# A new order for the opening of a fused attention and MLP kernel: the first split pair moves into it, two masks become two wide operations, the last store goes out in halves

## The chip, the cores and the metric

The kernel runs on one core of one Trainium2 chip. The metric is device time in microseconds (us) of one execution. Before the change the median of three runs is 651.92 us (651.72 to 652.86). The engines are called PE (TensorE, matmul), DVE (VectorE), ACT (ScalarE), POOL (GpSimd) and SP (SyncE, which here does nothing but issue DMAs); PEld is the weight load of PE.

## What is computed

Attention over 4 batches of 8 heads with 768 positions of 64 numbers, where a query sees the first 4 keys and a window of 128 keys back, and then a gated MLP on all 3072 tokens:

```python
scores = scale * np.matmul(q, k.transpose(0, 1, 3, 2))
keep = is_sink | in_window            # pos < n_sink, 0 <= rel < window
scores = np.where(keep, scores, -1000000000.0)
a = np.exp(scores - np.max(scores, axis=-1, keepdims=True))
a = a / (np.sum(a, axis=-1, keepdims=True) + 1e-09)
x = np.matmul(a, v)                   # then (3072, 512)
h = x @ w_in                          # 512 x 2048, float64 weights
g = h * np.clip(h + 3.0, 0.0, 6.0) / 6.0
out = (g @ w_out).astype(np.float32)  # 2048 x 512
```

`n_sink` and `window` are inputs. Where they exceed 16 and 128 a general path behind a branch at the kernel's end computes everything anew; with the values here the branch jumps over it.

## The kernel before

Work is cut into units of 256 positions of one batch (12 units, three of each batch) and pairs of heads, four to a unit, so that there are 48 pairs `s`. The first 16 pairs belong to the first unit of each batch. They are "plain": their scores are float32 matmuls on operands as loaded. The other 32 are "split": queries and keys are cut into a high and a low part (`split_parts`), and DMAs within the chip's own buffers stack the parts (`B_k`, `B_q`, eight DMAs a pair). A pair's steps are scores, masking and row minimum on DVE (`S_least`), exponential on ACT (`X_exp`), transposes on PE, a copy back on ACT or DVE (`T_copy`), and the product with the values (`E_plain`, `E_av`).

The MLP takes two units at once. Its 16 weight blocks are float64 in memory; each is loaded (`W_load`, 1 MB) and decoded in six steps of 128x1024 (`W_decode`): 1 and 2 on ACT, 3, 4 and 6 on DVE, 5 on the engine that a letter of `WHI` names. `PFE`, `XHS`, `XHF` and `GHF` name engines for other copies in the same way. Every product is made of three matmuls of 512 columns (high by high, high by low, low by high), `two_product` (line 690) and `two_second` (line 700) in six-matmul steps.

The opening is a list of some 900 steps written out, `FIRST`: p, q, u, l, v load, S are scores, M masking, X exponential, T transposes, C the copy, E the values, R, U, V, x, y the rest of a plain pair, W a weight load, w.j.k decode step k of block j, F, G and O the MLP of units 0 and 1 (products in, activation, products out), b the parts of x, i.n are n matmuls that nothing reads. Each engine, SP's DMA issue included, takes these steps in the order of the list. When a buffer that a DMA writes is still in use, SP stands at that DMA with all behind it.

After the list comes a loop of slots (line 872), one for each pair from `FROM` on. A slot's `ORDER` holds the steps of neighbouring pairs (c scores and softmax of the pair before, k and q splits of this one, d transposes, s sinks, e values of the pair two back, l and v loads) and eight letters f. Each f takes one six-matmul MLP step from a queue; a group of two units has 64 of them and eight pairs feed it. `SPARED` (line 861) takes f's out of a slot again: 2 of 8 from seven of the first nine slots, 1 from two. The scheduler may move instructions of the loop among each other; the opening stays as written.

The last steps are the four outputs of the last two units: ACT scales 128x512 out of PSUM (line 658), SP stores it (line 660). Then each engine reads a flag and jumps over the general path (line 904), and SP waits for all stores.

Of the kernel before, what the change touches and what calls it, by code (L numbers as in the profile page):

```python
# [44 lines left out]
def attn_ffn_kernel(ctx: ExitStack, tc: tile.TileContext, qx, kx, vx, px, vsx, limits, w_in, w_out, out):  # L45
    nc = tc.nc
    B, NU, NP = qx.shape[0:3]
# [46 lines left out]
    nc.sync.dma_start(out=raw.rearrange("p a b -> p (a b)"), in_=limits.bitcast(I32).partition_broadcast(P))  # L94
# [22 lines left out]
    def unless_sink(dst, bias):  # L117
        nc.vector.scalar_tensor_tensor(out=dst, in0=colf[:, 0:P], scalar=ns_f, in1=bias, op0=ALU.is_ge, op1=ALU.mult)
# [94 lines left out]
    GHF = "AADAAADADAAAADAD"  # L213
    WHI = "ADDDAADDDAADDDAD"
# [54 lines left out]
    PFE = "ADADDDDDDDADAAADDADDAADAAAAAAADA"  # L269
    XHS = "AAAAAAAADDADAAAA"  # L270
    XHF = "AAADADAAADADAAAA"
# [16 lines left out]
    def A_kq(s):  # L288
        b, u, p = pus[s]
        kr = work.tile([P, 400], F32, name="kr")  # L290
        qr = work.tile([P, UT], F32, name="qr")
        nc.sync.dma_start(out=kr[:, 0:ncol(u)], in_=kx[b, u, p, :, 0:ncol(u)])
        nc.sync.dma_start(out=qr, in_=qx[b, u, p])
        st_[s].update(kr=kr, qr=qr)

    def A_v(s):
# [7 lines left out]
        VS = work.tile([P, 3, 4 * D], F32R, name="VS")  # L304
        v4 = VS.rearrange("p s (h d) -> p s h d", h=4)
        vr = work.tile([P, 3, 2, D], F32, name="vr", bufs=1)
        nc.sync.dma_start(out=vr[:, 0:n], in_=vx[b, u, p, :, 0:n])
        split_parts(nc, v4[:, 0:n, 0::2, :], v4[:, 0:n, 1::2, :], vr[:, 0:n], nc.scalar, nc.vector)
        st_[s]["VS"] = VS

    def B_k(s):
# [6 lines left out]
        st_[s]["ktqt"], st_[s]["KQ"] = ktqt, work.tile([P, KQ], F32R, tag="K", name="K", bufs=1)  # L320
        K = st_[s]["KQ"][:, 0:1600].rearrange("p (h r w) -> p h r w", h=2, r=2)
        for h in range(2):
            for r in range(2):
                nc.sync.dma_start(out=K[D * r:D * (r + 1), h, :, 0:w].bitcast(F32),
                                  in_=kt[D * h:D * (h + 1), :, 0:w].bitcast(F32))
        st_[s]["K"] = K

    def B_q(s):
# [4 lines left out]
        split_parts(nc, qt[:, 0, :], qt[:, 1, :], d["qr"], eng(QHI, s), eng(QLO, s))  # L333
        Q = d["KQ"][:, 1600:KQ].rearrange("p (h t) -> p h t", h=2)
        for h in range(2):
            for r in range(2):
                nc.sync.dma_start(out=Q[D * r:D * (r + 1), h, :].bitcast(F32),
                                  in_=qt[D * h:D * (h + 1), r, :].bitcast(F32))
        d["Q"] = Q
# [309 lines left out]
    def ffn_out(tt, pool, acc, dst, final=False):  # L649
# [4 lines left out]
        elif pool is work:  # L654
            o = spare(0)[:, tt]
        else:
            o = pool.tile([P, DM], F32, name="ost")
        nc.scalar.mul(out=o, in_=acc, mul=1.0 / 6.0)
        if pool is work:
            nc.sync.dma_start(out=dst.rearrange("(s r) d -> r s d", s=2), in_=o)  # L660
        else:
            nc.sync.dma_start(out=dst, in_=o)

    def ffn_whole(x, pool, psum_h, psum_o, dsts):
# [11 lines left out]
        for tt in range(2):  # L676
            ffn_out(tt, pool, state[f"o{tt}"], dsts[tt])
# [15 lines left out]
    def two_second(n, j, one, state, tts=(0, 1)):  # L693
        gh, gl = (x.rearrange("p (t u) -> p u t", u=2)[:, one] for x in state[j])
        for tt in tts:
# [7 lines left out]
            if j == LAST - 1 and n:  # L703
                b, u = units[2 * n + one]
                r0 = b * S + u * UT + P * tt
                ffn_out(tt, work, acc, out[r0:r0 + P, :], 2 * n + one == len(units) - 1)
# [20 lines left out]
    def drain(n):  # L727
# [333 lines left out]
```

## Time and profile before

| | us |
|---|---|
| median of 3 runs | 651.92 |
| the profiled execution | 652.39 |
| its span, first to last instruction | 650.7 |
| PE busy | 640.5 (98%) |
| DVE busy | 491.3 (76%) |
| ACT busy | 414.6 (64%) |
| POOL busy | 180.0 (28%) |

The granted TensorE clock is 0.998 over the span, the upper of its two levels (2.4 GHz). Of the profiled execution, 1.7 us lie outside the span. A matmul's duration in the profile is longer than the step from one to the next, since they overlap, so a PE that is called busy can still lose time; how fast it goes is read from the count of matmuls in a stretch.

### The profile page before, as it was taken

Reading aid. Unit: us, or ns where it says so; the run is one execution under the profiler, and the core shown is the slowest. Engines: PE = TensorE matmul, PEld = TensorE weight load, DVE = VectorE, ACT = ScalarE, POOL = GpSimd, SP = SyncE. Lnnn points to the kernel's source line nnn. Section 1 sums busy time; section 2 is a strip of 40 time slices with the busy share of each in tenths; the row PEclk is TensorE's granted clock in tenths of the full one; section 3 lists DMA queues with packets and bytes.
Section 4 is the critical chain, followed back from the end, with each engine's and each line's share of the span. In section 5 each row is a group of like instructions: output and inputs, shape, how many; then the busy total and the mean of one; then the engine's idle time right before and its main releaser. Section 6 shows DMA issues by size and latency. Waiting matters only on the chain.

```text
span 650.7 us, 11572 instructions
## 1 busy us (share of the span) xinstructions
PE 640.5 (98%) x3556; PEld 574.3 (88%) x3556; DVE 491.3 (76%) x1290; ACT 414.6 (64%) x1046; POOL 180.0 (28%) x336
## 2 busy tenths in 40 slices
PE   8999999999999999999999999999999999999996
PEld 7898988888888889999998999999999999888885
DVE  5999999957887887977888878788788787433331
ACT  5978778645777788666777776678867765311111
POOL 1000000001454444454445434543354344000000
PEclk9999999999999999999999999999999999999999
DMA  8545940018665657544555555445754540100001
GB/s 320 208 172 215 380 154 1 2 56 212 169 164 138 177 137 205 142 116 120 128 139 145 169 132 136 117 116 137 196 129 104 121 105 2 64 1 1 0 2 70
DMA packets 45749, 82.93 MB, mean 127 GB/s; under 512 B 7024, under 2 KB 30832, under 8 KB 43632
## 3 DMA queue, kind: packets, MB, share of 16 engines
q1 hardware_dynamic: 45680, 82.11, 43.9%
q8 instruction: 31, 0.51, 0.3%
q14 instruction: 38, 0.31, 0.1%
HBM read 41.19 MB, written 6.29 MB: 73 GB/s over the span
## 4 chain that ended last, share of the span: by engine, by line
PE 92%; ACT 3%; DMA 2%; issue 1%; DVE 1%; SPq 0%; POOL 0%; ACTq 0%; DVEq 0%; POOLq 0%
PE o L700 35%; PE hps L690 34%; PE av L561 5%; PE sp L402 4%; PE av L532 3%; PE pt L496 2%; PE sp L371 2%; PE pt L478 2%; PE o L645 2%; PE hps L611 1%; DMA qr<-in_qx_dram 1%; ACT Pt L421 1%; PE idle L88 1%; DMA K<-kt 1%; DMA raw_s<-in_vsx_dram 1%
## 5 line engine op out<-in xcount | busy, mean ns | idle before, releaser
L690 PE MATMUL hps<-x,w 128*128 128x512 f32 x1104 | 263.5, 383 | 0.0
L700 PE MATMUL o<-w,gh 128*128 128x512 f32 x736 | 223.9, 384 | 0.0
L690 PEld LDWEIGHTS hps<-x,w 128*128 128x128 f32 x1104 | 201.1, 189 | 24.8 <-ACT xf L35 0.3
L700 PEld LDWEIGHTS o<-w,gh 128*128 128x128 f32 x736 | 137.3, 197 | 11.2 <-issue 0.3
L700 PE MATMUL o<-w,g 128*128 128x512 f32 x368 | 139.7, 380 | 0.0
L463 POOL TENSOR_TENSOR Pt<-Pt 128x256 f32<-128x256 f32 x64 | 53.5, 836 | 276.2 <-ACT Pt L421 276.2
L622 ACT ACTIVATE ost<-hps,three 128x512 f32<-128x512 f32 x80 | 54.9, 686 | 87.1 <-PE hps L690 86.5
L627 DVE SCALAR_TENSOR_TENSOR ost<-ost,hps 128x512 f32<-128x512 f32 x80 | 54.7, 684 | 55.9 <-ACT ost L622 55.1
L509 POOL TENSOR_SCALAR_AFFINE_SELECT ph<-ph 128x256 fp32r<-128x256 f32 x128 | 68.2, 534 | 54.9 <-ACT ph L35 54.8
L700 PEld LDWEIGHTS o<-w,g 128*128 128x128 f32 x368 | 72.4, 197 | 6.9
L384 DVE CUSTOM_DVE_ANT_0 Pt<-sp,m_t 128x272 f32<-128x272 f32 x128 | 53.5, 434 | 32.8 <-PE sp L402 26.9
L421 ACT ACTIVATE Pt<-Pt,nb 128x272 f32<-128x272 f32 x128 | 65.8, 514 | 13.2 <-DVE nb L384 12.9
L511 POOL TENSOR_SCALAR_AFFINE_SELECT ph<-ph 128x256 fp32r<-128x256 f32 x128 | 59.6, 466 | 35.1 <-DVE ph L30 29.6
L636 DVE TENSOR_TENSOR g<-ost,gh 128x512 fp32r<-128x512 f32 x80 | 65.4, 817 | 2.7
L409 ACT ACTIVATE Pt<-Pt,rc 128x144 f32<-128x144 f32 x128 | 46.0, 406 | 9.4 <-POOL Pt L463 4.7
L402 PE MATMUL sp<-K 128*128 128x272 f32 x256 | 41.8, 281 | 1.0 <-DMA K<-kt 0.4
L402 PEld LDWEIGHTS sp<-K 128*128 128x128 f32 x256 | 37.6, 190 | 3.8 <-issue 1.4
L561 PEld LDWEIGHTS av<-ph,VS 128*128 128x128 f32 x256 | 38.0, 190 | 3.2 <-issue 0.5
L561 PE MATMUL av<-ph,VS 128*128 128x256 f32 x256 | 39.0, 275 | 0.0
L41 DVE CAST gh<-ost 128x512 fp32r<-128x512 f32 x80 | 36.1, 452 | 2.5
L35 ACT ACTIVATE ph<-pt 128x256 fp32r<-128x256 f32 x64 | 24.6, 385 | 20.5 <-PE pt L496 19.6
L564 DVE TENSOR_TENSOR xf<-av,xf 64x256 f32<-64x256 f32 x64 | 26.6, 416 | 10.3 <-ACT xf L563 9.4
(107 smaller groups left out, 836.7 us busy)
## 6 DMA issues: line engine op xcount, KB each, us to landing
K<-kt SPq DMA_DIRECT2D x128, 200.0 KB, 3.5
K<-kt SPq DMA_DIRECT2D x128, 64.0 KB, 2.5
kr<-in_kx_dram SPq DMA_DIRECT2D x32, 200.0 KB, 2.5
vr<-in_vx_dram SPq DMA_DIRECT2D x32, 192.0 KB, 2.6
out_dram<-ost SPq DMA_DIRECT2D x22, 256.0 KB, 2.6
lent<-in_w_in_dram SPq DMA_DIRECT2D x5, 1024.0 KB, 9.2
qr<-in_qx_dram SPq DMA_DIRECT2D x40, 128.0 KB, 2.6
lent<-in_w_out_dram SPq DMA_DIRECT2D x5, 1024.0 KB, 9.6
```

The costliest lines, as they stand in the source:

```text
L384: nc.vector.tensor_tensor_reduce(out=cell(s, h, t, 0, w), in0=sp[:, 0:w], in1=m[:, 0:w], scale=-SCALE, scalar=3.0e38, op0=ALU.add, op1=ALU ...
L402: nc.tensor.matmul(out=sp[:, 0:w], lhsT=Q[:, h, t * P:(t + 1) * P], rhs=keys, start=(r == 0), stop=(r == 1))
L421: nc.scalar.activation(out=blk, in_=blk, func=AF.Exp, scale=-1.0, bias=d["nb"][:, i:i + 1], accum_out=d["sm"][:, i:i + 1])
L463: nc.gpsimd.tensor_tensor(out=both, in0=both, in1=prior, op=ALU.add)
L509: nc.gpsimd.affine_select(out=prior[i], in_=own[i], pattern=[[0, 2], [-1, P]], base=0, channel_multiplier=1, compare_op=ALU.is_gt, fill=0.0)
L511: nc.gpsimd.affine_select(out=own[i], in_=own[i], pattern=[[0, 2], [1, P]], base=0, channel_multiplier=-1, compare_op=ALU.is_ge, fill=0.0)
L561: nc.tensor.matmul(out=o, lhsT=l, rhs=r, start=(j == 0), stop=(j == len(seq) - 1))
L622: nc.scalar.activation(out=gf, in_=hp, func=AF.Relu, bias=three, scale=1.0)
L627: nc.vector.scalar_tensor_tensor(out=gf, in0=gf, scalar=6.0, in1=hp, op0=ALU.min, op1=ALU.mult)
L636: nc.vector.tensor_tensor(out=g, in0=gf, in1=gh.bitcast(F32), op=ALU.subtract)
L690: nc.tensor.matmul(out=state["h", j], lhsT=l(j // 2)[:, c, fs], rhs=r, start=(c == 0 and k == 0), stop=(c == NP - 1 and k == 2))
L700: nc.tensor.matmul(out=acc, lhsT=l[:, tt * P:(tt + 1) * P], rhs=r(j // 2)[:, j % 2, :].rearrange("p (s d) -> p d s", s=2), start=(j == 0 a ...
```

## The change

- The opening's list is new throughout: other positions for loads, decode steps and copies. `WHI` gives step 5 of 11 blocks to ACT instead of 6 (blocks 1, 2, 3 among the first four), `PFE` has 16 letters D instead of 15, `XHF` 6 instead of 4, `XHS` 3 and `GHF` 5 as before. There are 8 idle matmuls at the start instead of 10, and two more (i.2) between the first scores and the first transposes.
- The first split pair, 16, has its splits, stacking DMAs, values and sinks (K.16, Q.16, v.16, h.16) in the list, each cut into load or DMA (0), high part (1) and low part (2). The loop starts at 17 and holds pair 16's scores, transposes and products. The last four output steps of units 0 and 1, with their stores, move from the list's end to the head of the loop's queue (`LATE`). `SPARED` takes one f each out of two slots.
- The limits' DMA is issued by ACT, in front of its table load, instead of as SP's first. The four masks of the plain pairs are one tile, made by two operations of 256 columns instead of four of 128; POOL copies from it.
- The last of the 24 stores is scaled in halves of 256 columns on DVE and ACT and stored by two DMAs, from SP and from ACT.
- The general path loops over 16 pairs in place of four batches with eight heads written out, and its MLP loads and stores once a batch. Counted in the built program's order, SP's instructions behind the jump fall from 257 rows to 33, DVE's from 934 to 267, PE's from 470 to 291; ACT has 23 rows before and after. The inputs qx, kx and vx have two axes exchanged, with the same rows.

```diff
-WARM = (10, 16, 4)
+WARM = (8, 16, 4)
-def split_parts(nc, hi, lo, src, hi_engine, lo_engine):
-    copy_r(nc, hi_engine, hi, src)
-    lo_engine.tensor_tensor(out=lo, in0=src, in1=hi.bitcast(F32), op=ALU.subtract)
+def split_parts(nc, hi, lo, src, hi_engine, lo_engine, parts=(1, 2)):
+    if 1 in parts:
+        copy_r(nc, hi_engine, hi, src)
+    if 2 in parts:
+        lo_engine.tensor_tensor(out=lo, in0=src, in1=hi.bitcast(F32), op=ALU.subtract)
...
-    nc.sync.dma_start(out=raw.rearrange("p a b -> p (a b)"), in_=limits.bitcast(I32).partition_broadcast(P))
+    nc.scalar.dma_start(out=raw.rearrange("p a b -> p (a b)"), in_=limits.bitcast(I32).partition_broadcast(P))
...
-    outside(ownb, ahead, win_f)
-    unless_sink(m_00, ownb)
-    outside(prevb, behind, win_f)
-    unless_sink(m_01[:, 0:P], prevb)
+    outside(m_0[:, 2 * P:4 * P], relf[:, P:3 * P], win_f)
+    nc.vector.scalar_tensor_tensor(out=both(m_0[:, 0:2 * P]), in0=colf[:, 0:P].unsqueeze(1).to_broadcast([P, 2, P]),
+                                   scalar=ns_f, in1=both(m_0[:, 2 * P:4 * P]), op0=ALU.is_ge, op1=ALU.mult)
...
-    GHF = "AADAAADADAAAADAD"
-    WHI = "ADDDAADDDAADDDAD"
+    GHF = "AAAADADAAADADADA"
+    WHI = "AAAAADDDAAAAADAD"
...
+        if final and tt:
+            a, c = slice(0, DM // 2), slice(DM // 2, DM)
+            nc.vector.tensor_scalar(out=o[:, a], in0=acc[:, a], scalar1=1.0 / 6.0, scalar2=None, op0=ALU.mult)
+            nc.scalar.mul(out=o[:, c], in_=acc[:, c], mul=1.0 / 6.0)
+            nc.sync.dma_start(out=to[:, :, a], in_=o[:, a])
+            nc.scalar.dma_start(out=to[:, :, c], in_=o[:, c])
+            return
...
-    FROM = 16
+    FROM = 17
-        q.0 q.1 p.2 u.0 u.1 v.9 p.3 p.6 p.5 S.0.0 p.4 S.0.1 M.0.1.0 W.4 S.1.1 M.0.0.0 X.0.1.0 M.0.1.1 S.1.0
+        q.0 q.1 p.2 u.0 v.8 u.1 p.3 p.6 S.0.0 p.4 S.0.1 W.0 M.0.1.0 M.0.0.0 p.5 X.0.1.0 S.1.1 X.0.0.0 M.0.1.1
...
+    ready = {"K": B_k, "Q": B_q, "v": A_v, "h": sink_loads}
+        elif kind in ready and len(n) == 2:
+            ready[kind](n[0], (n[1],))
...
-    SPARED = {FROM + k: 2 if k % 5 else 1 for k in range(9)}
+    SPARED = {FROM + k: 1 for k in (3, 6)}
+    LATE = "O.0.7.0 O.0.7.1 O.1.7.0+o.0.0+o.0.1 O.1.7.1+o.1.0+o.1.1"
+    queues.append([lambda x=x: [first_step(y) for y in x.split("+")] for x in LATE.split()])
     queues.append(two_steps(1))
...
-            elif FROM <= at < NS:
+            elif FROM - (kind in "cdes") <= at < NS:
...
-            with tc.For_i(0, B, 1) as bi:
-                for a in range(NP):
-                    for h in range(2):
-                        head(bi, a, h)
+            with tc.For_i(0, B * NP, 1) as at:
+                pair_whole(at)
```

SP's first DMAs, before and then after. `lent` are the plain pairs' inputs (772, 512 or 260 columns) or weight blocks (2048 columns) in buffers that later hold decoded weights; `VF` and `kr`, `qr` are inputs of later pairs.

```order
L94 DMA raw<-in_limits_dram 128x4
L284 DMA lent<-in_px_dram 128x512 x2
L284 DMA lent<-in_px_dram 128x772
L284 DMA lent<-in_px_dram 128x260 x2
L301 DMA VF<-in_px_dram 128x260
L284 DMA lent<-in_px_dram 128x772 x4
L170 DMA lent<-in_w_in_dram 128x2048
```

```order
L284 DMA lent<-in_px_dram 128x512 x2
L284 DMA lent<-in_px_dram 128x772
L284 DMA lent<-in_px_dram 128x260
L301 DMA VF<-in_px_dram 128x260
L284 DMA lent<-in_px_dram 128x260
L284 DMA lent<-in_px_dram 128x772 x3
L169 DMA st<-in_w_in_dram 128x2048
L284 DMA lent<-in_px_dram 128x772
L169 DMA lent<-in_w_in_dram 128x2048
```

The limits are gone from SP, and the last row shown after, block 14, goes into the buffer that the first two pairs' inputs hold.

PE around the first split pair's scores (`sp<-K`) up to its first transposes (`pt<-ident_r,Pt`), before and then after; `hps` are products in, `o` products out.

```order
L402 MATMUL sp<-K 128x272 x4
L700 MATMUL o_1789<-w_1106,gh 128x512
L700 MATMUL o_1789<-w_1106,g 128x512
L402 MATMUL sp<-K 128x272 x2
L700 MATMUL o_1824<-w_1024,gh 128x512 x2
L700 MATMUL o_1824<-w_1024,g 128x512
L402 MATMUL sp<-K 128x272 x2
L690 MATMUL hps<-x_1623,w_725 128x512 x3
L496 MATMUL pt<-ident_r,Pt 128x128 x2
```

```order
L405 MATMUL sp<-K 128x272 x6
L706 MATMUL o_943<-w_1618,gh 128x512 x2
L706 MATMUL o_943<-w_1618,g 128x512
L405 MATMUL sp<-K 128x272 x2
L706 MATMUL o_981<-w_1618,gh 128x512 x2
L706 MATMUL o_981<-w_1618,g 128x512
L696 MATMUL hps<-x_1662,w_472 128x512 x3
L499 MATMUL pt<-ident_r,Pt 128x128 x2
```

Rows that repeat with another buffer are left out. Between the scores and the transposes stand now the outputs of units 0 and 1 (`o_943`, `o_981`) and the first product of units 2 and 3; before, outputs of units 2 and 3.

ACT at the end, before and then after, with what each instruction waits for; DVE's part of the last output precedes it.

```order
L658 ACTIVATE end<-o_7146 128x512 [waits PE_49]
L658 ACTIVATE end<-o_7150 128x512 [waits PE_49]
L903 TENSOR_LOAD flag_i [waits DVE_49]
L904 COMPARE_AND_BRANCH
```

```order
L667 ACTIVATE end<-o_7145 128x512 [waits PE_49]
L663 ACTIVATE end<-o_7149 128x256 [waits DVE_49]
L665 DMA out_dram<-end 64x2x256 [waits Activation_49]
L914 TENSOR_LOAD flag_i [waits DVE_49]
L915 COMPARE_AND_BRANCH
```

The last activation is half as wide and waits for DVE, not for PE.

## Rows read from the trace of the kernel before

**Rows 1.** The page: busy us of each engine, share of the span, instructions.
```profile
PE 640.5 (98%) x3556; PEld 574.3 (88%) x3556; DVE 491.3 (76%) x1290; ACT 414.6 (64%) x1046; POOL 180.0 (28%) x336
```

**Rows 2.** Stretches: start:end us, length, busy us and (instructions) by engine, clock, DMA.
```profile
20.00:60.00 40.00, 39.96 (x343) 37.04 (x342) 39.13 (x130) 33.72 (x67) 0.00 (x0) 1.00 0.43 150
150.00:240.00 90.00, 88.28 (x480) 77.07 (x479) 72.34 (x212) 65.92 (x203) 39.86 (x78) 1.00 0.63 164
240.00:550.00 310.00, 310.00 (x1699) 280.46 (x1699) 251.33 (x687) 223.66 (x638) 135.51 (x240) 1.00 0.50 130
```

**Rows 3.** Waits of PE: who for whom, total us, times, longest.
```profile
PE sp L371 <- DMA qr<-in_qx_dram: 0.5, 1, 0.5
```

**Rows 4.** Stretches of line 690's instructions alone: PE and PEld, busy us (count).
```profile
152.95:241.24 88.29, 37.75 (x156) 28.04 (x156) 1.00 0.63 163
267.22:358.05 90.83, 37.92 (x157) 28.04 (x156) 1.00 0.52 132
```

**Rows 5.** The same stretches, line 700's instructions alone.
```profile
152.95:241.24 88.29, 36.83 (x141) 25.71 (x140) 1.00 0.63 163
267.22:358.05 90.83, 44.13 (x180) 33.56 (x180) 1.00 0.52 132
```

**Rows 6.** The chain in order of time: start us, us, what.
```profile
175.63 0.56 PE av L561 x5
...
636.72 7.78 PE o L700 x36
```

**Rows 7.** Timeline of the start: start us, us, engine, line, operation, count [idle before, releaser].
```profile
0.81 0.39 SPq L94 DMA_DIRECT2D raw<-in_limits_dram  x1
1.21 4.64 PE L88 MATMUL idle<-rel 128*128 128x128 f32 x20 [1.21 <-POOL rel L65]
1.26 2.31 SPq L284 DMA_DIRECT2D lent<-in_px_dram  x5
5.22 0.35 DVE L118 SCALAR_TENSOR_TENSOR m<-col,nw,m_t 128x128 bf16<-128x128 f32 x1
5.77 1.69 PE L371 MATMUL sp<-lent 64*128 64x128 f32 x16
7.91 0.84 PE L478 MATMUL pt<-ident_r,Ph 128*128 128x128 f32 x5 [0.19 <-ACT Ph L419]
```

**Rows 8.** DMA issues: what, engine, count, KB each, median us to landing.
```profile
qr<-in_qx_dram SPq DMA_DIRECT2D x40, 128.0 KB, 2.6
lent<-in_px_dram SPq DMA_DIRECT2D x2, 256.0 KB, 3.5
out_dram<-end SPq DMA_DIRECT2D x2, 256.0 KB, 2.9
lent<-in_w_out_dram SPq DMA_DIRECT2D x5, 1024.0 KB, 9.6
```

**Rows 9.** Groups by shape, 0 to 160 us: count, busy us, mean ns, idle before.
```profile
L41 DVE CAST w<-wt 128x1024 fp32r<-128x1024 f32 x10 | 6.8, 684 | 0.0
L35 ACT ACTIVATE w<-wt 128x1024 fp32r<-128x1024 f32 x6 | 6.4, 1067 | 1.9 <-DVE wt L205 1.9
L41 DVE CAST x<-xp 128x256 fp32r<-128x256 f32 x2 | 0.8, 417 | 0.0
L35 ACT ACTIVATE x<-xp 128x256 fp32r<-128x256 f32 x6 | 2.2, 366 | 0.0
```

**Rows 10.** Timeline of ACT at the end.
```profile
644.53 0.60 ACT L658 ACTIVATE end<-o 128x512 f32<-128x512 f32 x1 [0.70 <-PE o L700]
```

**Rows 11.** Line 904, the jump: engine, operation, ns min/median/max, first and last start us.
```profile
L904 SPq EVENT_SEMAPHORE  x8: 17/17/17, 648.8 to 649.3; - x8
L904 ACTq COMPARE_BRANCH  x1: 50/50/50, 645.1 to 645.1; - x1
L904 ACTq EVENT_SEMAPHORE  x1: 17/17/17, 645.5 to 645.5; - x1
L904 SPq COMPARE_BRANCH  x1: 50/50/50, 645.7 to 645.7; - x1
```

More of the change, by code (lines that the diff above doesn't have):

```diff
@@ L268, in attn_ffn_kernel @@
     NLENT = 8
-    PFE = "ADADDDDDDDADAAADDADDAADAAAAAAADA"
-    XHS = "AAAAAAAADDADAAAA"
-    XHF = "AAADADAAADADAAAA"
+    PFE = "DDDAADDDAAAAAADDDAAAAADAAADDDDDD"
+    XHS = "AAAAAAAAAADDAADA"
+    XHF = "DADAAAAADADADDAA"
     def plain(s):
@@ L303, in A_v @@
             return
[L304 to L313, printed above, removed]
+        if 0 in parts:
+            st_[s]["vr"] = work.tile([P, 3, 2, D], F32, name="vr", bufs=1)
+            nc.sync.dma_start(out=st_[s]["vr"][:, 0:n], in_=vx[b, p, u, :, 0:n])
@@ L326, in B_k @@
-        st_[s]["K"] = K
-    def B_q(s):
+        d, w = st_[s], ncol(pus[s][1])
+        if 1 in parts:
+            d["ktqt"] = work.tile([P, KTQT], F32R, tag="kt", name="kt", bufs=1)
+        kt = d["ktqt"][:, 0:800].rearrange("p (r w) -> p r w", r=2)
+        split_parts(nc, kt[:, 0, 0:w], kt[:, 1, 0:w], d["kr"][:, 0:w], eng(KHI, s), eng(KLO, s), parts)
+        if 0 in parts:
+            d["KQ"] = work.tile([P, KQ], F32R, tag="K", name="K", bufs=1)
+            K = d["K"] = d["KQ"][:, 0:1600].rearrange("p (h r w) -> p h r w", h=2, r=2)
+            for h in range(2):
+                for r in range(2):
+                    nc.sync.dma_start(out=K[D * r:D * (r + 1), h, :, 0:w].bitcast(F32),
+                                      in_=kt[D * h:D * (h + 1), :, 0:w].bitcast(F32))
@@ L329, in B_q @@
+    def B_q(s, parts=(0, 1, 2)):
         if plain(s):
@@ L332, in B_q @@
         qt = d["ktqt"][:, 800:KTQT].rearrange("p (r t) -> p r t", r=2)
[L333 to L339, printed above, removed]
+        split_parts(nc, qt[:, 0, :], qt[:, 1, :], d["qr"], eng(QHI, s), eng(QLO, s), parts)
+        if 0 in parts:
+            Q = d["Q"] = d["KQ"][:, 1600:KQ].rearrange("p (h t) -> p h t", h=2)
+            for h in range(2):
+                for r in range(2):
+                    nc.sync.dma_start(out=Q[D * r:D * (r + 1), h, :].bitcast(F32),
+                                      in_=qt[D * h:D * (h + 1), r, :].bitcast(F32))
     def spans(u):
@@ L705, in two_second @@
                 r0 = b * S + u * UT + P * tt
-                ffn_out(tt, work, acc, out[r0:r0 + P, :], 2 * n + one == len(units) - 1)
+                ffn_out(tt, acc, out[r0:r0 + P, :], 2 * n + one == len(units) - 1)
     def two_steps(n):
@@ L809, in unit_step @@
             r0 = b * S + u * UT + P * i
-            ffn_out(i, work, state[f"o{i}"], out[r0:r0 + P, :])
+            ffn_out(i, state[f"o{i}"], out[r0:r0 + P, :])
     def first_step(step):
@@ L967, in head @@
-                    xo = pg.tile([P, P], F32, tag="pgt", name="pgt")
-                    for j in range(NTL):
-                        nc.tensor.matmul(out=xo[0:D, :], lhsT=gv[:, j, :], rhs=pT[:, j, :],
-                                         start=(j == 0), stop=(j == NTL - 1))
-                    nc.vector.tensor_copy(out=xT[:, t * P:(t + 1) * P], in_=xo[0:D, :])
-                nc.sync.dma_start(out=xdv[ds(bi, 1), a, h].rearrange("o d s -> (o d) s"), in_=xT)
-            with tc.For_i(0, B, 1) as bi:
-                for a in range(NP):
-                    for h in range(2):
-                        head(bi, a, h)
@@ L992, in attn_ffn_kernel @@
-                    ffn_whole([xb[:, c] for c in range(NP)], gp, pg, pf, dsts)
+                    split_parts(nc, xb[:, :, 0], xb[:, :, 1], xn[:, :, u * UT:(u + 1) * UT], nc.vector, nc.vector)
+                    ffn_whole([xb[:, c] for c in range(NP)], gp, pg, pf, ost[:, 2 * u:2 * u + 2])
+                nc.sync.dma_start(out=ov[ds(bi, 1)].rearrange("o t p e -> (o p) t e"), in_=ost)
 _OUTS = [((3072, 512), 'float32')]
```

261 lines of the change are left out of this document (130 added, 131 removed).

## The prediction

> **What bounds the kernel now.** I read the page first: PE is busy 640.5 of 650.7 us [rows 1], so the change can win only what PE loses at the start, at the end and between matmuls. Then the stretches: PE's idle time in them is 0.04 us from 20 to 60, nothing from 240 to 550, but 1.72 us from 150 to 240 [rows 2]. Since a busy PE can still lose time, I count matmuls. The step of one 512-column matmul is 7.78/36 = 0.216 us [rows 6]. In seven steady slots, 267.22 to 358.05, lines 690 and 700 run 336 of them (157 + 180, less one that both edges cut) in 90.83 us [rows 4, 5]. A slot is 12.98 us, 48 x 0.216 = 10.37 of it MLP and 2.60 the attention part of one pair. The joint before that, from the first scores of pair 16 (152.95) to those of pair 24 (241.24), is 88.29 us long and holds 296 such matmuls (156 + 141, less one): 296 x 0.216 = 63.9, and eight attention parts of 2.60 = 20.8, less the ten value matmuls that its first slot has not got (two groups of five at 0.56 [rows 6], 1.1): 83.6. So PE loses 4.7 us there, though it shows 1.7 us idle. Eight slots of eight f's would hold 384; the joint is thin because `SPARED` takes f's out, and a thin slot leaves less matmul work in front of each wait for the softmax or for stacked keys.
>
> The start: the ten idle matmuls end at 5.85 and the first scores stand at 5.77 [rows 7]. The end: ACT scales the last output from 644.53 to 645.13 [rows 10], its store lands 2.9 us after the issue [rows 8], and SP passes its first wait behind the jump at 648.8, 1.9 us before the span ends [rows 11].
>
> **The change part by part**, against the profiled execution of 652.39 us, which is 0.47 above the median.
>
> Start. The limits leave SP's queue, so the first input is issued at 0.81 instead of 1.26 and lands at 0.81 + 3.5 = 4.3 [rows 7, 8]. Two idle matmuls fewer are 4 of 20 records, 4.64 x 4/20 = 0.93 us, measured by their step 0.85. The first scores then start near 4.9, which is behind the landing. ACT issues the limits at about the time SP did and its table load follows; ACT is not needed before 6. The masks end at 5.57 now [rows 7]; two wide operations can hardly end later than four narrow ones, and scores that start at 4.9 ask for them near 5.6. But i.2 gives 0.85 back on PE. It stands in front of the five transposes at 7.91, where PE now waits for ACT's `Ph` [rows 7], so a part of it fills time that is lost anyway, and I count the middle. I take -0.4, ends -0.85 (i.2 covers what would be idle) and 0.
>
> Opening. All matmuls stay, and their order changes hardly any cost that I can see; what can change is who is late. From 20 to 60 DVE is busy 39.1 of 40 us and ACT 33.7 [rows 2]. Five casts of 128x1024 move to ACT: DVE is relieved of 5 x 0.684 = 3.4 and gets one more `PFE` and two more `XHF` copies (2 x 0.417, and for the `PFE` copy the middle between 0.417 and 0.684, 0.55), net -2.0; ACT pays 5 x 1.067 = 5.3, of which three blocks, 3.2 us, come among the first four decoded, against 40 - 33.7 = 6.3 us of slack there [rows 2, 9]. The one long wait that PE shows, 0.5 us for an input of pairs 11 and 12 [rows 3], goes, since their loads stand further ahead in SP's list. A new order can have a wait of its own. Ends: -2.0 (all that DVE is relieved of) to +3.2 (all of ACT's early casts in front of PE); nearest to the row of the wait, -0.5.
>
> Joint. Pair 16's splits and DMAs go where ACT and DVE have slack (150 and earlier), slot 16 goes, and the f's taken out fall from sixteen to two. Nine slots then hold 70 f's for 68 steps, so seven of them are like the steady slot that loses nothing. The loss now is 4.7 us over about eight slots, 0.6 each, nearly all of it with six f's; for the two slots with seven I take half, 0.3 each. The first slot has four scalings of outputs on ACT (0.60 each [rows 10]) and four stores on SP among the softmax and the stacking, for which I take another 0.9. That leaves 1.5 of 4.7: -3.2; ends -4.7 and 0. SP's queue there holds kr, qr, vr loads, eight stacking DMAs a pair and now four stores; a late stacking DMA would show as scores waiting.
>
> End. By the halves alone nothing is won: the order shows ACT's half waiting for DVE's. A copy of 256 columns out of PSUM is 0.42 us on DVE and 0.37 on ACT [rows 9], 0.79 in a row against 0.60 now, so ACT's half leaves 0.2 later, but the store is of 128 KB (2.6 against 2.9 [rows 8]): landing about equal, near 648.1. The short general path is worth more. SP jumps at 645.7 and goes on at 648.8, ACT jumps at 645.1 and goes on at 645.5 [rows 11]: SP has 257 rows to jump over, ACT 23. With 33 rows SP should go on like ACT, pass the waits of stores long landed at once, and reach the last one, at 648.1, with about 1.5 of the 1.9 us left: 649.6 against 650.7, -1.1. I take -0.9; ends -1.4 and +0.3 (the later half as long under way as a whole store).
>
> Two rules of the Trainium skill bear on this. Page PSUM — Partial Sum Buffer, section PSUM bank collisions raise a hardware error: two engines may not access one bank and quadrant at once, reads included, so the halves of one bank must go one after the other, as the order has them; were it not so, 0.42 in place of 0.79 would make the end 0.4 us earlier. Page Runtime: NRT & Kernel Launch, section Instruction fetch mechanics: a taken branch whose target is outside the prefetched window waits for a fetch; by that rule SP's 3.1 us are a fetch and go away (the -1.1), and if they were the wait for the last landing instead (645.13 + 2.9 = 648.0), the end would win only 0.2.
>
> Sum: -0.4 - 0.5 - 3.2 - 0.9 = -5.0, that is 647.4 against the profiled execution and 646.9 against the median of 651.92.
>
> **The rivals.**
> ACT becomes the bound of the opening. For it: the 3.2 us above, and that ACT takes its list in order, so that its slack is not all of use. Against it: DVE, at 98%, is the one that is relieved. The time is 646.9 + 3.2 + 0.5 = 650.6 with the wait not gone either; still faster.
> The joint does not gain. If what it loses comes from the stacking DMAs (eight a pair on one queue) and not from missing f's, the loss goes along: 646.9 + 3.2 = 650.1. Against it: steady slots have the same DMAs and lose nothing.
> Slower: SP stands at block 14. That DMA goes into the buffer of the first two pairs, so SP waits until PE is through with them, near 15 us, and pair 7's inputs and block 2 stand behind it; before, all of SP's first 21 DMAs were free to go early. All 16 blocks pass through DVE, which has 0.9 us to spare from 20 to 60 [rows 2]; each us that block 2 is late beyond that is paid in full. It decides from 6.3 us (5.0 won and 1.3). If a whole weight load comes late, 9.6 us [rows 8], the time is 646.9 + 9.6 - 0.9 = 655.6. Against it: block 2 is the fourth to be loaded and its transfer would end near 24, about when it is decoded.
>
> **How the numbers follow.** No change means within 0.2%, 1.3 us, which is about what a measurement of this kernel can tell. Forecast as above 0.68; ACT in the opening 0.15; the joint keeps its loss 0.10; slower 0.07. Faster by over 1.3 us, below 650.6: 0.68 + half of the second case + most of the third + nothing of the last = 0.86; within: 0.08; slower: 0.06. All the good ends together are -0.85 - 2.0 - 4.7 - 1.4 = -9.0, 643; the forecast's own range is 644.8 to 648.8. To hold 8 in 10 it must reach into the second and third cases: 644.7 to 650.4.
>
> **What would show it.** Right: first scores near 4.9; no 0.5 us wait for qr near 61; pair 16's scores to pair 24's holding 372 matmuls at no more than 2 us over 372 x 0.216 + 19.7; SP's first wait behind the jump below 647 and the span's end within 1.6 us of the last landing. Wrong: PE waiting for ACT between 20 and 60, or for loads in front of pair 7 or block 2; scores in the joint waiting for `K<-kt`; SP still 3 us behind its jump.

## The result and the profile after

The changed kernel takes 657.73 us (median of 6 runs, 656.90 to 658.55), the kernel before 651.92: a ratio of 1.0088 (95% interval 1.0075 to 1.0101). It is slower by 5.8 us, where 5.0 us less were forecast. The profiled execution's span is 656.0 us against 650.7.

In what follows a matmul's loss is its start minus the start of the one before it, less the median step behind a matmul of that earlier one's shape in the kernel before (0.216 us for 512 columns). A start that comes sooner than that counts as negative, so that the differences add up to the 5.3 us between the two spans. Summed by stretches this gives, in us, with the end as the time from PE's last start to the end of the span:

| stretch | before | after | difference | forecast |
|---|---|---|---|---|
| 0 to 150 us (start and opening) | 4.5 | 6.8 | +2.4 | -0.9 |
| 150 to 240 (joint) | 4.7 | 0.1 | -4.6 | -3.2 |
| 240 to PE's last start (loop) | 0.2 | 7.3 | +7.1 | 0 |
| from there to the end | 6.58 | 7.03 | +0.45 | -0.9 |

Of the 2.4 us in the first row, 1.9 lie between 60 and 100 us.

The page's busy time, answering to [rows 1], tells nothing of this: PE is still at 98%.

```profile
PE 642.8 (98%) x3556; PEld 574.7 (88%) x3556; DVE 483.3 (74%) x1287; ACT 409.9 (62%) x1048; POOL 168.5 (26%) x337
```

The stretches do, beside [rows 2] (length, then busy us and count of PE, PEld, DVE, ACT, POOL, clock, DMA). From 150 to 240 PE has no idle time left. From 240 to 550 it shows 3.93 us idle where it had none, and 1663 matmuls where 1699 stood.

```profile
150.00:240.00 90.00, 90.00 (x495) 81.49 (x494) 71.22 (x199) 64.22 (x189) 36.39 (x70) 1.00 0.54 142
240.00:550.00 310.00, 306.07 (x1663) 274.41 (x1662) 237.78 (x673) 208.59 (x620) 121.22 (x236) 1.00 0.51 130
```

The joint in the prediction's own measure, line 696 and then line 706 alone, from pair 16's first scores (141.48) to pair 24's (241.54), answering to [rows 4, 5]: 192 + 181, less one cut by the edge, are the 372 matmuls that were named, and 372 x 0.216 + 19.7 = 100.05 is all of the length of 100.06. It loses nothing.

```profile
141.48:241.54 100.06, 46.49 (x192) 34.56 (x192) 1.00 0.55 143
...
141.48:241.54 100.06, 43.87 (x181) 33.49 (x180) 1.00 0.55 143
```

What PE waits for after (engine, line, waited for: total us, times, longest), beside the one row of [rows 3]. The wait for qr is gone, as forecast. The first and the last of the four rows are new and come three times each; the second (1.2) is the same before; the third has grown from the row shown below them, which is of the kernel before.

```profile
PE sp L405 <- DVE ost L630: 2.7, 3, 1.3
PE idle L90 <- POOL rel L67: 1.2, 1, 1.2
PE pt L481 <- ACT Ph L422: 1.1, 2, 0.8
PE hps L696 <- ACT x L37: 0.8, 3, 0.3
```

```profile
PE pt L478 <- ACT Ph L419: 0.2, 1, 0.2
```

**The loop.** The three places are at 242, 348 and 454 us, eight slots apart, where a group of eight pairs ends and the parts of its x are made. The stretches of 20 us there (240 to 260, 340 to 360, 450 to 470) hold 6.9 of the loop's 7.3 us; 3.5 of them stand in the two rows of waits, and how the rest divides was not told apart. The timeline of the second (start, length, engine, line, operation, count, idle before), DVE and PE:

```profile
343.38 1.54 PE L696 MATMUL hps<-x,w 128*128 128x512 f32 x6
344.67 1.50 DVE L591 TENSOR_TENSOR x<-xf,x 128x256 fp32r<-128x256 f32 x3
346.43 0.64 DVE L591 TENSOR_TENSOR x<-xf,x 128x256 fp32r<-128x256 f32 x1
347.00 0.90 DVE L43 CAST x<-xf 128x256 fp32r<-128x256 f32 x2
347.47 0.63 PE L405 MATMUL sp<-K 128*128 128x272 f32 x4
347.82 0.95 DVE L591 TENSOR_TENSOR x<-xf,x 128x256 fp32r<-128x256 f32 x2
348.69 0.68 DVE L630 SCALAR_TENSOR_TENSOR ost<-ost,hps 128x512 f32<-128x512 f32 x1
349.42 0.50 PE L405 MATMUL sp<-K 128*128 128x272 f32 x2 [1.33 <-DVE ost L630]
351.05 0.43 DVE L387 CUSTOM_DVE_ANT_0 Pt<-sp,m_t 128x272 f32<-128x272 f32 x1
```

The first row is the last product in of the old group. Eight parts of x stand on DVE in front of line 630, which is the last reader of a product in. Scores and products share the PSUM banks (one pool tag), so the next scores wait 1.33 us for that reader; the minimum of the first scores starts 3.6 us after them. The same place before: six of the parts come in front of the first minimum, other work of DVE between them, the minimum follows the scores by 1.4 us, and PE does not wait.

```profile
343.17 0.53 DVE L41 CAST x<-xf 128x256 fp32r<-128x256 f32 x1 [0.15 <-PE hps L690]
343.68 1.51 PE L690 MATMUL hps<-x,w 128*128 128x512 f32 x6
343.73 1.05 DVE L588 TENSOR_TENSOR x<-xf,x 128x256 fp32r<-128x256 f32 x2
345.02 0.86 PE L402 MATMUL sp<-K 128*128 128x272 f32 x6
345.53 0.28 DVE L41 CAST x<-xf 128x256 fp32r<-128x256 f32 x1
345.73 0.75 DVE L588 TENSOR_TENSOR x<-xf,x 128x256 fp32r<-128x256 f32 x2
346.40 0.43 DVE L384 CUSTOM_DVE_ANT_0 Pt<-sp,m_t 128x272 f32<-128x272 f32 x1
```

Why the order differs: a group has 64 MLP steps and its eight slots 64 f's, so whatever is left in the queue when a group's last pair is done is left at every later group too. Before, nine slots from 16 on with 16 f's out, and four f's of the next, make 9 x 8 - 16 + 4 = 60 of 64 steps: four are left. After, 8 x 8 - 2 + 4 = 66 of 4 + 64: two are left. The last product in, which frees x for the next group, falls two f's earlier: before, PE takes it (343.68) right in front of the scores (345.02); after (343.38), the twelve matmuls of two steps of products out stand between it and the scores (347.47), and DVE has come to the parts of x by then.

**The start.** The limits' DMA, issued by ACT at the time when SP issued it before, is used by DVE at 5.26 and not at 3.70, and the first minimum stands at 6.86 where it stood at 6.43, though the scores start earlier (5.10) than in [rows 7]. The first inputs are slower too: they are issued 0.45 us earlier, but land 4.5 us after their issue, where [rows 8] has 3.5.

```profile
0.82 0.41 ACTq L96 DMA_DIRECT2D raw<-in_limits_dram  x1
5.26 0.16 DVE L98 SCALAR_TENSOR_TENSOR neg<-raw 128x2 f32<-128x2 int32 x1 [4.28 <-DMA raw<-in_limits_dram]
6.86 0.29 DVE L387 CUSTOM_DVE_ANT_0 Ph<-sp,m 128x128 f32<-128x128 f32 x1 [0.15 <-PE sp L374]
```

```profile
lent<-in_px_dram SPq DMA_DIRECT2D x2, 256.0 KB, 4.5
```

**The opening.** SP stands until 80.2 at the keys of pair 15, whose buffer is still read, and block 8 behind them is issued at 81.0. ACT waits for it until 88.24, its exponentials come behind that decode step, and PE waits for them at 91.1 and again at 93.4.

```profile
76.57 0.42 SPq L301 DMA_DIRECT2D VF<-in_px_dram  x1
80.17 0.33 SPq L292 DMA_DIRECT2D kr<-in_kx_dram  x1
...
81.03 0.42 SPq L169 DMA_DIRECT2D lent<-in_w_in_dram  x1
...
88.24 1.29 ACT L193 ACTIVATE wt<-lent 128x1024 f32<-128x1024 f32 x1 [2.44 <-DMA lent<-in_w_in_dram]
...
90.69 0.39 ACT L422 ACTIVATE Ph<-Ph,nb 128x128 f32<-128x128 f32 x1
...
91.14 0.55 PE L481 MATMUL pt<-ident_r,Ph 128*128 128x128 f32 x3 [0.78 <-ACT Ph L422]
```

**The end.** Line 915 is the jump, line 1067 the closing barrier (ns min/median/max, first and last start), beside [rows 11]. SP now goes on 0.5 us behind its jump, as forecast. But ACT, which issues a DMA of its own first, reads the flag and jumps only at 652.2, and comes to its DRAIN in the barrier at 655.1, 1.0 us after SP's. The span ends 2.6 us after SP has passed the last landing (653.4), where 1.6 had been named.

```profile
L915 SPq EVENT_SEMAPHORE  x8: 17/17/17, 651.0 to 653.4; - x8
...
L915 SPq COMPARE_BRANCH  x1: 50/50/50, 650.5 to 650.5; - x1
L915 ACTq COMPARE_BRANCH  x1: 54/54/54, 652.2 to 652.2; - x1
...
L1067 SPq DRAIN  x3: 7/7/7, 654.0 to 655.5; - x3
...
L1067 ACTq DRAIN  x2: 8/72/135, 655.1 to 655.5; - x2
```

### The profile page after: what moved, and what is told of

Its sections match the earlier page's. It is cut to its first block, busy times and chain, and to the rows that moved or that the text cites. A ratio compares the mean times of both kernels' runs of the same rounds, so it can differ in the third digit from the quotient of the medians.

```text
span 656.0 us, 11554 instructions
## 1 busy us (share of the span) xinstructions
PE 642.8 (98%) x3556; PEld 574.7 (88%) x3556; DVE 483.3 (74%) x1287; ACT 409.9 (62%) x1048; POOL 168.5 (26%) x337
## 4 chain that ended last, share of the span: by engine, by line
PE 80%; DVE 7%; ACT 7%; DMA 3%; issue 2%; POOL 0%; SPq 0%; DVEq 0%; ACTq 0%
PE hps L696 31%; PE o L706 29%; PE av L564 4%; PE sp L405 3%; PE av L535 3%; ACT Pt L424 3%; PE sp L374 2%; PE pt L481 2%; PE hps L614 2%; PE o L648 2%; PE pt L499 2%; DVE x L591 1%; ACT Pt L412 1%; DMA lent<-in_w_in_dram 1%; DMA vr<-in_vx_dram 1%
## 5 line engine op out<-in xcount | busy, mean ns | idle before, releaser
L696 PE MATMUL hps<-x,w 128*128 128x512 f32 x1104 | 266.6, 383 | 1.0 <-ACT x L37 0.8
L466 POOL TENSOR_TENSOR Pt<-Pt 128x256 f32<-128x256 f32 x64 | 48.2, 754 | 266.2 <-ACT Pt L424 266.2
L512 POOL TENSOR_SCALAR_AFFINE_SELECT ph<-ph 128x256 fp32r<-128x256 f32 x128 | 59.4, 464 | 71.5 <-ACT ph L37 71.5
L514 POOL TENSOR_SCALAR_AFFINE_SELECT ph<-ph 128x256 fp32r<-128x256 f32 x128 | 61.9, 484 | 47.7 <-DVE ph L32 40.9
L639 DVE TENSOR_TENSOR g<-ost,gh 128x512 fp32r<-128x512 f32 x80 | 60.3, 754 | 1.8
L387 DVE CUSTOM_DVE_ANT_0 Pt<-sp,m_t 128x272 f32<-128x272 f32 x128 | 50.7, 428 | 2.8 <-PE sp L405 2.5
L450 DVE RECIPROCAL rc<-sm 128x2 f32<-128x2 f32 x64 | 10.5, 164 | 44.1 <-ACT sm L449 44.1
L43 DVE CAST gh<-ost 128x512 fp32r<-128x512 f32 x80 | 38.6, 482 | 1.7
```

The lines of the kernel that those rows point to most:

```text
L387: nc.vector.tensor_tensor_reduce(out=cell(s, h, t, 0, w), in0=sp[:, 0:w], in1=m[:, 0:w], scale=-SCALE, scalar=3.0e38, op0=ALU.add, op1=ALU ...
L512: nc.gpsimd.affine_select(out=prior[i], in_=own[i], pattern=[[0, 2], [-1, P]], base=0, channel_multiplier=1, compare_op=ALU.is_gt, fill=0.0)
L514: nc.gpsimd.affine_select(out=own[i], in_=own[i], pattern=[[0, 2], [1, P]], base=0, channel_multiplier=-1, compare_op=ALU.is_ge, fill=0.0)
L639: nc.vector.tensor_tensor(out=g, in0=gf, in1=gh.bitcast(F32), op=ALU.subtract)
L696: nc.tensor.matmul(out=state["h", j], lhsT=l(j // 2)[:, c, fs], rhs=r, start=(c == 0 and k == 0), stop=(c == NP - 1 and k == 2))
```

## The experiments

Ratios are to the kernel before on the same chip (medians there 652.0 to 652.6, against 651.92 beside the changed kernel, so a gain read from the times alone is uncertain by some 0.6 us; by the ratios the gains told below, 6.6 for the f's, 2.0 for block 8, 1.6 for the limits, 1.0 and 1.6 for the two last stores, are 7.0, 2.3, 1.6, 1.1 and 2.0).

**Four f's out: four steps left.**
```diff
-    SPARED = {FROM + k: 1 for k in (3, 6)}
+    SPARED = {FROM + k: 1 for k in (1, 3, 5, 7)}
```


> The changed kernel with four f's taken out in place of two (one each from slots 18, 20, 22 and 24), so that four MLP steps are still in the queue when a group's last pair is done, as before the change, and not two. Theory of the queue's lead: the 6.9 us that the stretches around 245, 350 and 460 us lost against the kernel before come from the shift of the last product in by two f's, which puts seven parts of x on DVE in front of the next scores' minimum. Then these three waits go and the time falls from 657.7 by 6 to 7 us, less up to 0.6 for two more thin slots: 651 to 652. Rival, the new engine letters of x (XHS) or the joined pair make these places slow: the time stays within 1 us of 657.7.


651.09 us, ratio 0.9981 (0.9972 to 0.9990): 6.6 less than the changed kernel, and faster than the kernel before. PE's waits for line 630 and for x are gone, and the loop loses 1.0 us in place of 7.3:

```profile
PE pt L481 <- ACT Ph L422: 1.1, 3, 0.5
...
PE hps L696 <- ACT kt L37: 0.6, 1, 0.6
```

The second row is one wait, at 367 us, taken up below.

**The same shift in the kernel before: two steps left.**
```diff
-    SPARED = {FROM + k: 2 if k % 5 else 1 for k in range(9)}
+    SPARED = {FROM + k: 2 if k % 5 and k not in (3, 6) else 1 for k in range(9)}
```


> The kernel before with 14 f's taken out in place of 16 (two slots give one f and not two), nothing else changed, so that two steps are left as in the changed kernel. Theory of the queue's lead: the three places of 2.2 to 2.9 us appear here too, and two thin slots less win up to 0.6 to 1: 651.9 + 6 to 7, about 657.5 to 658.5. Rival, the new list or its letters are the cause: the time stays at 651 to 652.


657.17 us, ratio 1.0076 (1.0063 to 1.0090). The old list and the old letters give the same waits; in the profile the loop loses 7.3 us more, the joint 1.9 and the start 0.8 less.

```profile
PE sp L402 <- DVE ost L627: 3.3, 4, 1.3
...
PE hps L690 <- ACT x L35: 0.8, 3, 0.3
```

**Six f's out.**
```diff
+    SPARED = {FROM + k: 1 for k in (1, 2, 3, 5, 6, 7)}
```


> The changed kernel with six f's taken out (one each from slots 18, 19, 20, 22, 23 and 24), so that six steps are left. Theory of the queue's lead: what counts is where the last product in falls in a slot; here it falls behind the scores, the parts of x stand behind the minimum on DVE, and PE loses nothing at the three places or as little as with four left; two more thin slots cost up to 0.6: 651 to 653. If instead only the exact place of the kernel before is good, the three places lose again 2 us each: 656 to 658.


661.50 us, ratio 1.0139 (1.0123 to 1.0154): above both forecasts and worse than two; the loop loses 11.0 us, with the waits below, again three times each. ACT waits there 1.8 us in two pieces (235 to 265 us) in front of an output's scaling for the store that last read its buffer, with the softmax behind it. So more steps in the queue are not simply better; the old place was a good one. Of the three numbers tried, four costs least. That ACT's wait is what makes six worse is read from this one profile, and no run tested it.

```profile
PE pt L499 <- ACT Pt L412: 3.3, 3, 1.3
PE av L564 <- DVE nb L387: 2.5, 3, 1.0
PE sp L405 <- DVE ost L630: 1.6, 3, 0.5
```

**The low parts of x on POOL, two steps left.**
```diff
-            nc.vector.tensor_tensor(out=x[:, 1, one], ...)
+            (nc.gpsimd if s >= 4 * NP else nc.vector).tensor_tensor(out=x[:, 1, one], ...)
```


> The changed kernel with the low part of x (the subtraction of 128x256) of all pairs from 16 on made by POOL and not by DVE; the queue's lead stays at two. Theory: the scores at 242, 348 and 454 us wait because some seven parts of x stand on DVE ahead of their minimum; with five to seven of them gone these waits (0.5 to 1.3 us in the profile, 0.7 to 1.5 by matmul starts, 3.2 together) go, while the products in behind them still wait for x (0.8 each) or, POOL being the slower engine, longer: 653.5 to 656.5. Rival, it is not DVE's queue but the arrival of the keys or the products' own place that makes the scores late: no gain, 657 to 660.


660.10 us, ratio 1.0111 (1.0095 to 1.0127): a miss, at the upper end of the rival's range. The half that was argued holds, the scores' wait for line 630 (2.7) is gone and 0.9 for the minimum is left. But the products in wait 3.9 us in place of 0.8, which is more than was won; that price had only been guessed (a part takes POOL 0.74 us in this profile, DVE 0.42).

```profile
PE hps L696 <- ACT x L37: 2.7, 3, 0.9
...
PE hps L696 <- POOL x L591: 1.2, 3, 0.4
PE sp L405 <- DVE nb L387: 0.9, 2, 0.6
```

**Block 8 ahead of pair 15.**
```diff
-        X.14.0.1 T.13.0 l.15 F.0.3.0 C.13.0 w.7.1 C.13.1 W.8 E.13.0
+        X.14.0.1 T.13.0 W.8 l.15 F.0.3.0 C.13.0 w.7.1 C.13.1 E.13.0
```


> The changed kernel with the load of weight block 8 moved in front of the loads of pair 15 in the list, nothing else changed. Theory: SP stands from 77 to 80 us at pair 15's keys, whose buffer the scores of pair 13 or 14 still read, block 8 is issued at 81.0 behind it and lands at 88.2, ACT waits 2.4 us for it, and PE waits for ACT at 90 to 93.5 (0.94 + 0.53 + 0.29 us). With the load ahead it is issued near 77, lands near 84, and the time falls by 1.5 to 1.8 us to 656. Rival, ACT simply has too many casts in the opening: its wait goes, but PE still waits, and the time stays within 0.5 us of 657.7.


655.75 us, ratio 1.0053 (1.0039 to 1.0067): 2.0 less. The block is issued at 76.94 in place of 81.03, ACT's decode step and the exponential behind it come 1.8 us earlier, and PE waits for the exponentials 0.2 us in place of 1.1.

```profile
76.94 0.42 SPq L169 DMA_DIRECT2D lent<-in_w_in_dram  x1
80.06 0.33 SPq L292 DMA_DIRECT2D kr<-in_kx_dram  x1
...
86.36 1.53 ACT L193 ACTIVATE wt<-lent 128x1024 f32<-128x1024 f32 x1 [0.67 <-DMA lent<-in_w_in_dram]
...
88.85 0.39 ACT L422 ACTIVATE Ph<-Ph,nb 128x128 f32<-128x128 f32 x1
```

**The limits on SP.**
```diff
-    nc.scalar.dma_start(out=raw.rearrange(...), ...)
+    nc.sync.dma_start(out=raw.rearrange(...), ...)
```


> The changed kernel with the limits' DMA issued by SP as its first again, nothing else changed. Theory: on ACT the limits came 1.5 us later (DVE starts on them at 5.26 against 3.70 before), so the masks end at 6.7 against 5.57 and DVE's first minimum stands at 6.86 against 6.43; with SP the masks end near 5.5 again, the first input is issued 0.45 later and lands near 5.3, and the first minimum stands near 6.3: 0.3 to 0.6 us faster, 657.2. Rival, the late inputs cost what the masks win: within 0.2 us of 657.7.


656.16 us, ratio 1.0063 (1.0049 to 1.0076): 1.6 less, more than expected. The masks are made 1.3 us earlier, and the scores do not start later (4.92 against 5.10), since the first inputs, issued 0.45 us later, land 3.6 us after their issue and not 4.5.

```profile
3.97 0.16 DVE L98 SCALAR_TENSOR_TENSOR neg<-raw 128x2 f32<-128x2 int32 x1 [2.99 <-DMA raw<-in_limits_dram]
5.64 0.29 DVE L387 CUSTOM_DVE_ANT_0 Ph<-sp,m 128x128 f32<-128x128 f32 x1 [0.21 <-PE sp L374]
```

**The last store: both halves from SP, and whole.** The first replaces ACT's `dma_start` of the second half by SP's, the second scales whole on ACT and stores whole from SP.

> The changed kernel with both halves of the last store issued by SP, none by ACT. Theory: ACT's own DMA makes it late (it reads the flag at 650.98 to 652.12, jumps at 652.2, and comes to the last barrier only at 655.07, while SP is there at 654.03); without it ACT is at the barrier before 652, the last landing stays near 653.4, and the span ends 1.0 to 1.2 us earlier: 656.6. Rival, ACT is late there whatever it issues: the time stays at 657.7.

> The changed kernel with the last output scaled whole on ACT and stored whole by SP, as before the change; the short general path stays. Theory: landing as with the halves, within 0.3 us, and ACT early at the barrier, so 0.9 to 1.3 us faster than the changed kernel, 656.5 to 656.8. From PE's last matmul to the span's end this takes 6.2 to 6.6 us, against 6.6 in the kernel before: the short path wins at most 0.4. If the jump was worth the 1.1 us of the prediction, it takes 5.5.


656.78 us (1.0071, 1.0057 to 1.0084) and 656.15 us (1.0058, 1.0045 to 1.0072): 1.0 and 1.6 less than the changed kernel. From PE's last start to the end of the span it takes 6.15 and 5.65 us, after 7.03 and 6.58 before. By these profiles the short general path alone is worth 0.9 of the 1.1 forecast, the halves cost 0.5, and ACT's DMA another 0.9. Each is one profile, and the other runs bound it: the four kernels with the whole store take 5.65 to 6.04, the seven with ACT's DMA 5.95 to 7.03 (5.95 and 5.96 in two with four f's out, 6.71 or more in the other five). So the path is worth 0.5 to 0.9, and the halves with ACT's DMA cost up to 1.4 together; how that divides between the two rests on one run. The rows of the whole store:

```profile
L915 ACTq COMPARE_BRANCH  x1: 45/45/45, 650.0 to 650.0; - x1
...
L1067 SPq DRAIN  x3: 7/7/7, 653.9 to 654.2; - x3
...
L1067 ACTq DRAIN  x2: 8/72/136, 653.1 to 654.2; - x2
```

ACT is as long behind its jump as after the change (3.1 against 2.9 us), but it jumps 2.3 us earlier with respect to PE's last matmul, and is at the barrier before SP.

**The repairs together.** First the f's and block 8; then all four; then with `XHS` of the kernel before, for the one wait of a product in for ACT that four f's out leave; then that kernel with the limits on ACT again.

> The changed kernel with four f's taken out and with block 8's load ahead of pair 15's: the two repairs together. If they are independent, as the theories of the queue's lead and of SP's wait have it, the gains of 6.6 and 2.0 us add up: 649.1. Rival, they share a cause (a busy ACT or DVE that both repairs relieve): 650 to 651.

> The changed kernel with all four repairs: four f's out, block 8 ahead of pair 15, the limits on SP, the last store whole from SP. If the four losses are independent their gains add up: 657.7 - 6.6 - 2.0 - 1.6 - 1.6 = 646.0, and from PE's last matmul to the end it takes 5.6 us. Rival, the head's gain is hidden behind a later wait of the opening: 647.5.

> The kernel with the four repairs, and with the letters of x (XHS) of the kernel before. With four f's out one wait of 1.0 us is left, of a product in for ACT's part at 364 us, in the one group whose letters the change moved. Theory: with the old letters it goes, as it is absent in the kernel before: 0.8 to 1.0 us less than the four repairs alone, 645.0. Rival, it comes from something else: the same time as with the four repairs alone.

> The kernel with the four repairs and the old letters of x, but with the limits' DMA issued by ACT as in the changed kernel. Theory: the limits on ACT end the masks 1.0 to 1.2 us later in every execution, and nothing behind hides it: the ratio to the kernel before rises from 0.9920 to 0.9935 to 0.9940, about 648.5 where the kernel before takes 652.3. Rival, the opening takes the loss up in a later wait: the ratio stays within 0.0005 of 0.9920.


| kernel | us | ratio (95% interval) |
|---|---|---|
| f's and block 8 | 649.30 | 0.9956 (0.9943 to 0.9970) |
| all four | 648.79 | 0.9947 (0.9929 to 0.9964) |
| all four, old `XHS` | 647.55 | 0.9920 (0.9904 to 0.9935) |
| the same, limits on ACT | 648.95 | 0.9943 (0.9929 to 0.9957) |

The first two gains add up; the four do not, 648.8 and not 646.0. In the profiles the first repairs' kernel ends 5.96 us after PE's last start though ACT still stores, because ACT is there only 1.8 us behind its jump, 0.1 us before SP: most of the end's gain is taken in already (5.72 with all four). That does not explain all of it: from the first row to the second the profiled spans lose 1.3 us (647.6 to 646.3), the medians 0.5, and the six runs of the second row spread over 2.2 us, so the rest stays open. With the old letters the wait is gone and the loop loses 0.4 us in place of 1.3. The start's gain shows in the last row (1.4 us). The kernel with the old letters beats both kernels of this case; its waits of PE hold only the row of the idle matmuls at the start, 1.2 us.

## Why the prediction was wrong

The direction was wrong because the sum had no term for the loop. The step that failed is in the joint: "the f's taken out fall from sixteen to two. Nine slots then hold 70 f's for 68 steps". It counted f's for the joint alone, took the later slots as losing nothing because they lost nothing before, and never asked where the steps left over would put the last product in of each group. The two experiments on `SPARED`, one in each kernel, show the answer: the loop, put at 0, loses 7.1 us more, and two f's are worth 6.6 us one way and 4.9 (7.3 lost in the loop, 1.9 won back in the joint, 0.8 at the start, which the edit does not touch) the other. The order of the built kernel, with the parts of x on DVE in front of line 630, could have been read in advance; I had looked at pair 16's slots only.

- Joint: right in kind, and in the matmul count exact. The term was too small, -3.2 for -4.6: slots with one f out lose hardly anything, and four scalings and stores in the first slot cost nothing that the profile shows (0.9 had been taken off).
- Start: -0.4 forecast; it costs. "ACT issues the limits at about the time SP did" was right of the issue and wrong of the landing, and the first input did not land at 0.81 + 3.5 but 4.5 us after its issue. In the profile the first minimum comes 0.4 us later; against the limits on SP it is 1.2 us, and 1.4 to 1.6 in the times. The kernel before had a slow start in its profile, which hid part of it: its 20 idle matmul records step by 0.21 us to the last, and the scores start at 5.77; with two steps left, the start being the same code, the last six step by 0.11 and the scores start at 5.08. The granted clock reads 1.00 in both, and why they differ is not shown.
- Opening: qr's wait went, and ACT's additional casts hold up hardly anything between 20 and 60 us (PE is busy all of that stretch and loses 0.9 us there, 0.5 before), so that rival fell. The slower rival was right in kind, SP standing at a DMA with a weight block behind it, and wrong in place and size: at pair 15's keys, not at block 14, with 4.1 us of delay for the block, 1.7 of PE's losses and 2.0 of the time.
- End: the jump was right, 3.0 us to 0.5 on SP, forecast at 1.1 and worth 0.5 to 0.9 in the kernels with the whole store. In the Trainium skill, page Runtime: NRT & Kernel Launch, section Instruction fetch mechanics, a taken branch out of the prefetched window waits for a fetch; SP's rows agree with that (3.0 us, then 0.5). ACT's do not settle it, as told at the end. The comparison with ACT's 23 rows was not sound, for rows merge repeats: in the built programs the jump passes over 197 instructions of ACT before and 121 after, and 379 and 97 of SP. The halves were put at nothing; with ACT's DMA they cost up to 1.4, since all engines meet in the barrier and I followed SP alone. No run scaled the two halves at the same time.

With the four repairs and the old letters of x the kernel runs at 0.9920 of the kernel before, 646.7 on its 651.92, where 646.9 was forecast. That the two agree is luck in good part: this kernel no longer has the limits on ACT, the halves or only two f's out, and the terms differ from the forecast ones. Against the kernel before its joint wins 4.1 us (3.2 forecast), its end 0.7 (0.9), and start and opening together lose 0.15 where 0.9 was to be won (one profile of each, and the start of the kernel before varies by 0.8 between two). So the gain of the joint was there, and that of the start and opening is not shown.

## What to carry to other kernels

When slots of a loop and steps of a queue have the same period, any change at the loop's head moves every later group: count what is left in the queue at a group's end, before and after, and read the order of the built kernel at that place, not only at the place of the edit. A change in a list is priced by what stands behind each waiting DMA on its queue, all the way, not by the first one. At the end of a kernel follow every engine to the last barrier, since the one that was idle before may be last after.

## What the runs showed of the hardware

- A DMA of two numbers for each partition, issued at 0.8 us, is used by DVE at 3.7 to 4.0 us in the five profiles where SP issues it ahead of the inputs, and at 5.1 to 5.4 in the nine where ACT issues it beside them. The first two inputs (256 KB each, issued by SP) are later there, too: they land 3.5 to 3.6 us after their issue in the five and 4.3 to 4.5 in the nine, which takes away more than the 0.45 us won at the issue. Whether it is ACT's queue or the inputs in flight that delays the small one was not told apart.
- ACT's hole behind its jump, 1.8 to 3.4 us from the jump to its DRAIN in the barrier, comes in every kernel with the short path, though that path has fewer instructions for ACT to jump over (121, 197 before). The long path shows it or not: the kernel before took 0.5 in its profile and 2.7 with only two f's moved. It lies sometimes right behind the jump, sometimes one instruction later. Whether it is a fetch, as SP's rows suggest for SP, stays open: no run changed the place of ACT's code alone.
